# Loading the first x tile ahead of the weights, with the first products dealt out anew, in a fused convolution and two-matmul kernel

## The chip, the cores and the metric

The kernel runs on one core of one Trainium2 chip. The metric is device time in microseconds (us). A core has five engines that matter here: TensorE (PE in the profile, PEld for its weight loads), VectorE (DVE), ScalarE (ACT), GpSimd (POOL) and SyncE (SP), which issues most of the transfers. Times within a trace are microseconds from the start of the profiled execution, whose span is 1.7 to 2.1 us shorter than the time on the device in the runs here.

Before the change the median of three runs was 821.86 us (821.55 to 822.88).

## The reference, cut to what matters

```python
w = softmax(weight_gen, axis=-1)             # [8, 4096, 8 heads, 7 taps]
x_pad = pad x with 6 rows of zeros in front  # [8, 4096, 192] -> causal
conv[b, s, h] = sum over k of w[b, s, h, k] * x_pad[b, s + k, h]   # 24 channels per head
h = conv.reshape(32768, 192) @ w_in          # 192 -> 2048
out = (h - tanh(h)) @ w_out                  # 2048 -> 192
```

## The kernel before

The 32,768 tokens are cut into 32 superblocks of 1,024 tokens. For each superblock:

- a softmax of the tap weights (an exponential on ScalarE, sum and reciprocal on VectorE, a normalising product `wsm` on GpSimd);
- seven products of x with one tap each (`prod`, L146);
- transposes of these products on TensorE, which also add the seven taps up in PSUM (`pc`), and a copy to `convT` on ScalarE;
- 16 rounds, coded as 8 pairs, of a first matmul (`ph`, L192), a tanh on ScalarE and a subtraction on VectorE (`gt`, L203);
- the second matmul (`po`, L223), which runs one superblock behind.

"Body n" is below the loop's pass in which the first matmul of superblock n runs. The products of superblock n + 2 are made during body n. The parts that the change touches:

```python
    def products(n, on_vector=()):
        ...                                  # wsm on GpSimd
        for k in range(K):
            prod = ppool.tile([P, NC, J, H, GC], BF16, name=f"prod{k}", tag=f"prod{k}")
            eng = nc.vector if k in on_vector else nc.gpsimd
            eng.tensor_mul(prod..., x_t[:, k : k + J, :]..., wsm[:, :, :, k : k + 1]...)
    ...
    load(0)                                  # tap weights, then x, on SyncE's queue
    for h in range(H):                       # casts fp32 -> bf16, triggered by GpSimd
        nc.gpsimd.dma_start(out=w_in[h * GC : (h + 1) * GC], in_=moe_w_in...)
    softmax_exp(0)
    softmax_norm(0)
    products(0, on_vector=(1, 3, 5, 6))
    nc.sync.dma_start(out=w_in[R:P], in_=w_in[0:R])      # second copy, for the other half of the rows
    load(1)
    nc.gpsimd.dma_start(out=w_out[:], in_=moe_w_out...)
    softmax_exp(1)
    softmax_norm(1)
    conv(0, (0, 1))                          # transposes of superblock 0
    conv(0, (2,))
    products(1, on_vector=(2, 5))
    load(2)
    softmax_exp(2)
    softmax_norm(2)
    for n in range(NTOT):
        ...                                  # load(n + 3), products(n + 2)
        for p in range(J):
            gemm1(n, 2 * p)
            gemm1(n, 2 * p + 1)
            ...
            if n >= 1:
                gemm2((n - 1) * J + p)
            if n + 1 < NTOT:
                if p == (2 if n else 5):
                    conv(n + 1, (0, 1))
                if p == (5 if n else 6):
                    conv(n + 1, (2,))
            ...
```

x and the prods have two buffers each. Three PSUM buffers are shared by `ph` and `pc`.

The softmax here doesn't subtract the row's maximum and nothing guards it: scores larger than these inputs give would overflow.

## Time and profile before

| | before |
|---|---|
| time, median | 821.86 us |
| TensorE busy | 769.5 us, 94% of the span |
| GpSimd / VectorE / ScalarE busy | 82% / 81% / 78% |
| first x tile landed | 14.54 us |
| last product of superblock 0 | 29.55 us |
| first subtraction on VectorE | 38.98 us |
| GpSimd's last product of superblock 1 / of superblock 2 | 49.29 / 70.36 us |
| transposes of superblock 2 done | 70.95 us |

How to read it: an average over the whole span says "TensorE, 94%". That is true of bodies 2 to 31. It says nothing on the first 70 us, where TensorE waits for data. A change at the start can only move the point from which TensorE is full, and for this the question is what comes last there. "The transposes of superblock 2" means here and below the first of their two calls, `conv(2, (0, 1))`, which takes two thirds of the channels; the last third follows about 8 us later. The lines themselves are in the prediction below.

### The profile page before, as it was taken

The page shows a single profiled execution, that of the slowest core. Times are in us where ns is not written, and L with a number is a line of the kernel's source. Part 1 is how long each engine was busy: PE and PEld are TensorE (multiplying, and loading weights), DVE is VectorE, ACT ScalarE, POOL GpSimd, SP SyncE. Part 2 cuts the span into 40 slices and gives each one's busy share as a digit, 9 for nine tenths or more (in the row PEclk, how much of TensorE's full clock was granted, in tenths as well). Part 3 has the DMA queues.
Part 4 walks back from the last instruction along what each step waited for, and adds up shares of the span by engine and source line. Part 5 has one row for each costly group of instructions (what it writes and reads, how often), then busy time and mean ns, then how long its engine had stood idle before and what let it go on. Part 6 is the DMA issues. An engine that isn't in the chain of part 4 may idle for free.

```text
span 820.7 us, 35994 instructions
## 1 busy us (share of the span) xinstructions
PE 769.5 (94%) x16640; PEld 602.6 (73%) x16640; DVE 661.0 (81%) x591; ACT 640.1 (78%) x865; POOL 669.0 (82%) x265
## 2 busy tenths in 40 slices
PE   0379999999999999999999999999999999999997
PEld 0247777777778777777777777777777878777777
DVE  3987878888888887887888888888888888787783
ACT  0277778888888878888888888888888888888883
POOL 5999999998898888899888889988888898885000
PEclk9989999999999999999999999999999999999999
DMA  8823333233224323332333332233233223301112
GB/s 145 216 80 81 119 120 119 71 119 120 96 77 119 120 70 120 102 94 95 119 102 87 120 120 73 99 119 114 76 120 110 95 87 120 108 3 42 41 41 79
DMA packets 17286, 81.21 MB, mean 99 GB/s; under 512 B 4160, under 2 KB 8816, under 8 KB 12984
## 3 DMA queue, kind: packets, MB, share of 16 engines
q1 hardware_dynamic: 14560, 77.34, 28.2%
q0 software_dynamic: 2576, 1.57, 1.7%
q8 instruction: 130, 2.13, 1.1%
q14 instruction: 20, 0.16, 0.1%
HBM read 54.49 MB, written 25.17 MB: 97 GB/s over the span
## 4 chain that ended last, share of the span: by engine, by line
PE 79%; DVE 13%; ACT 4%; issue 2%; DMA 1%; SPq 0%; POOL 0%; ACTq 0%; DVEq 0%; POOLq 0%
PE ph L192 36%; PE po L223 35%; DVE gt L203 10%; PE pc L169 6%; ACT th L201 4%; DVE prod L146 3%; DMA x_t<-in_x_dram 1%; PE po L264 1%; DVE zr L129 0%; DVE zsum L125 0%; POOL wsm L136 0%; SPq L96 0%; ACT e_t L115 0%; SPq L100 0%; SPq L77 0%
## 5 line engine op out<-in xcount | busy, mean ns | idle before, releaser
L203 DVE TENSOR_TENSOR gt<-ph,th 128x1024 bf16<-128x1024 f32 x512 | 602.5, 1219 | 130.0 <-ACT th L201 130.0
L146 POOL TENSOR_TENSOR prod<-x_t,wsm 128x1536 bf16<-128x1536 f32 x218 | 632.6, 2939 | 78.0 <-issue 70.3
L201 ACT ACTIVATE th<-ph 128x1024 f32<-128x1024 f32 x512 | 496.9, 1022 | 58.3 <-PE ph L192 56.3
L192 PE MATMUL ph<-convT,w_in 64*128 64x512 bf16 x3072 | 393.1, 378 | 13.8 <-DVE gt L203 10.5
L223 PEld LDWEIGHTS <-gt 64*128 64x128 bf16 x7936 | 346.1, 94 | 54.4 <-issue 3.4
L223 PE MATMUL po<-w_out,gt 64*128 64x192 bf16 x7936 | 375.8, 243 | 4.2 <-issue 2.4
L192 PEld LDWEIGHTS <-w_in 64*128 64x128 bf16 x3072 | 171.3, 94 | 128.5 <-issue 38.1
L169 PE MATMUL pc<-ident,prod 64*128 64x64 bf16 x5376 | 93.7, 192 | 29.4 <-POOL prod L146 25.9
L169 PEld LDWEIGHTS <-prod 64*128 64x128 bf16 x5376 | 89.8, 96 | 31.2 <-POOL prod L146 26.2
L179 ACT ACTIVATE convT<-pc 128x1024 bf16<-128x1024 f32 x64 | 51.9, 810 | 65.0 <-PE pc L169 65.0
L248 ACT ACTIVATE out_sb<-po 128x192 f32<-128x192 f32 x248 | 82.5, 333 | 24.3 <-PE po L223 20.7
L115 ACT ACTIVATE e_t<-wg_t 128x448 f32<-128x448 f32 x32 | 18.5, 577 | 20.9 <-DMA wg_t<-in_weight_gen_dram 20.9
L136 POOL TENSOR_TENSOR wsm<-e_t,zr 128x448 f32<-128x448 f32 x32 | 31.1, 972 | 1.7 <-DVE zr L129 1.7
L146 DVE TENSOR_TENSOR prod<-x_t,wsm 128x1536 bf16<-128x1536 f32 x6 | 21.0, 3556 | 10.8 <-DMA x_t<-in_x_dram 9.6
L125 DVE TENSOR_REDUCE zsum<-e_t 128x64 f32<-128x448 f32 x32 | 19.5, 609 | 2.8 <-ACT e_t L115 2.8
L129 DVE RECIPROCAL zr<-zsum 128x64 f32<-128x64 f32 x32 | 17.7, 553 | 3.4 <-DVE zsum L125 0.5
L264 PE MATMUL po<-w_out,gt 64*128 64x192 bf16 x256 | 11.0, 243 | 0.0
L264 PEld LDWEIGHTS <-gt 64*128 64x128 bf16 x256 | 10.8, 93 | 0.0
L276 DVE TENSOR_TENSOR out_sb<-po,ot 128x192 f32<-128x192 f32 x8 | 2.9, 357 | 8.9 <-ACT ot L275 8.9
L275 ACT ACTIVATE ot<-po 128x192 f32<-128x192 f32 x8 | 2.6, 330 | 7.9 <-PE po L264 7.9
L292 POOL DMA_DIRECT2D w_in<-in_moe_w_in_dram x8 | 4.8, 604 | 0.4 <-issue 0.4
L115 ACT ACT_TABLE_LOAD x1 | 1.3, 1283 | 0.7 <-PEq L346 0.7
(8 smaller groups left out, 2.4 us busy)
## 6 DMA issues: line engine op xcount, KB each, us to landing
x_t<-in_x_dram SPq DMA_DIRECT2D x24, 1344.0 KB
out_dram<-out_sb SPq DMA_DIRECT2D x31, 768.0 KB
x_t<-in_x_dram SPq DMA_DIRECT2D x8, 1176.0 KB
wg_t<-in_weight_gen_dram SPq DMA_DIRECT2D x32, 224.0 KB
x_t<-in_x_dram SPq DMA_DIRECT2D x8, 157.5 KB
w_in<-in_moe_w_in_dram POOLq DMA_DIRECT2D x8, 96.0 KB, 11.2
w_in<-w_in SPq DMA_DIRECT2D x1, 768.0 KB
w_out<-in_moe_w_out_dram POOLq DMA_DIRECT2D x1, 768.0 KB, 13.0
```

The source lines that it names most:

```text
L115: nc.scalar.activation(out=e_t[:].rearrange("p j h k -> p (j h k)"), in_=wg_t[:].rearrange("p j h k -> p (j h k)"), func=ACT.Exp,)
L125: nc.vector.reduce_sum(out=zsum[:], in_=e_t[:].rearrange("p j h k -> p (j h) k"), axis=AX.X)
L136: nc.gpsimd.tensor_mul(wsm[:].rearrange("p j h k -> p (j h) k"), e_t[:].rearrange("p j h k -> p (j h) k"), zr[:].rearrange("p (n o) -> p n ...
L146: eng.tensor_mul(prod[:].rearrange("p c j h g -> p j h c g"), x_t[:, k : k + J, :].rearrange("p j (h c g) -> p j h c g", h=H, c=NC), wsm[: ...
L169: nc.tensor.matmul(pc[:, r, col : col + R], lhsT=prods[k][r * R : (r + 1) * R, c, 2 * j : 2 * j + 2].rearrange("p j h g -> p (j h g)"), rh ...
L179: nc.scalar.activation(out=convT[:, c0 : c0 + nch, :].rearrange("p c (j r t) -> p r (c j) t", r=2, t=R), in_=pc[:, :, 0 : nch * JH * R].re ...
L192: nc.tensor.matmul(ph[:, r, :], lhsT=w_in[r * R : (r + 1) * R, c, f * P : (f + 1) * P], rhs=convT[r * R : (r + 1) * R, c, :], start=(c == ...
L201: last_act[0] = nc.scalar.activation(out=th[:], in_=ph_f, func=ACT.Tanh)
L203: nc.vector.tensor_sub(gt[:], ph_f, th[:])
L223: mm = nc.tensor.matmul(po[:, 0:D], lhsT=g_of[n][f][r * R : (r + 1) * R, col : col + P], rhs=w_out[r * R : (r + 1) * R, f, :], start=(r == ...
L248: last_act[0] = nc.scalar.activation(out=out_sb[:, j, :], in_=po[:, 0:D], func=ACT.Copy)
L264: nc.tensor.matmul(po[:, r, 0:D], lhsT=g_of[n][f][r * R : (r + 1) * R, col : col + P], rhs=w_out[r * R : (r + 1) * R, f, :], start=(f == 0 ...
```

## The change

The intent is a shorter start. x of superblock 0 no longer moves beside w_in; GpSimd triggers w_in after its first product; the loads of superblock 1 go ahead of the copy of w_in to the other half of the rows; VectorE takes five instead of four of the first seven taps; to let VectorE start its subtractions sooner, all taps of superblock 1 go to GpSimd, and as they come later, the transposes of superblock 1 move behind the last pair of body 0. That copy of w_in is cut in two, so that its first half can start when half of w_in is there.

```diff
--- before.py
+++ after.py
@@ -129,7 +129,7 @@
         nc.vector.reciprocal(zr[:], zsum[:])
         zr_of[n] = (e_t, zr)
 
-    def products(n, on_vector=()):
+    def products(n, on_vector=(), between=None):
         x_t = x_of.pop(n)
         e_t, zr = zr_of.pop(n)
         wsm = wgpool.tile([P, J, H, K], FP32, name="wsm")
@@ -151,6 +151,8 @@
                 .to_broadcast([P, J, H, NC, GC]),
             )
             prods.append(prod)
+            if between is not None and k == 0:
+                between()
         prods_of[n] = prods
 
     def conv(n, chunks):
@@ -287,23 +289,29 @@
 
     ctx.enter_context(tc.manual_schedule())
 
+    def load_w_in():
+        for h in range(H):
+            nc.gpsimd.dma_start(
+                out=w_in[h * GC : (h + 1) * GC],
+                in_=moe_w_in[h * G : (h + 1) * G].rearrange("(c g) f -> g c f", c=NC),
+            )
+
     load(0)
-    for h in range(H):
-        nc.gpsimd.dma_start(
-            out=w_in[h * GC : (h + 1) * GC],
-            in_=moe_w_in[h * G : (h + 1) * G].rearrange("(c g) f -> g c f", c=NC),
-        )
     softmax_exp(0)
     softmax_norm(0)
-    products(0, on_vector=(1, 3, 5, 6))
-    nc.sync.dma_start(out=w_in[R:P], in_=w_in[0:R])
     load(1)
+    products(0, on_vector=(1, 3, 4, 5, 6), between=load_w_in)
+    for q in range(2):
+        nc.sync.dma_start(
+            out=w_in[R + q * R // 2 : R + (q + 1) * R // 2],
+            in_=w_in[q * R // 2 : (q + 1) * R // 2],
+        )
     nc.gpsimd.dma_start(out=w_out[:], in_=moe_w_out.rearrange("(c p) e -> p c e", c=NFT))
     softmax_exp(1)
     softmax_norm(1)
     conv(0, (0, 1))
     conv(0, (2,))
-    products(1, on_vector=(2, 5))
+    products(1)
     load(2)
     softmax_exp(2)
     softmax_norm(2)
@@ -320,9 +328,9 @@
             if n >= 1:
                 gemm2((n - 1) * J + p)
             if n + 1 < NTOT:
-                if p == (2 if n else 5):
+                if p == (2 if n else 7):
                     conv(n + 1, (0, 1))
-                if p == (5 if n else 6):
+                if p == (5 if n else 7):
                     conv(n + 1, (2,))
             if p == 2 and n + 3 < NTOT:
                 softmax_norm(n + 3)
```

## The prediction

> **What bounds the kernel now.** I read the page first, for what bounds the long middle; then the chain of waits, for where the start is lost; then GpSimd's timeline, because the change moves work to it; then stretches of the first 80 us with the granted clock.
>
> ```profile
> PE 769.5 (94%) x16640; PEld 602.6 (73%) x16640; DVE 661.0 (81%) x591; ACT 640.1 (78%) x865; POOL 669.0 (82%) x265
> PE   0379999999999999999999999999999999999997
> ```
>
> TensorE is above 90% busy from the fourth of 40 slices (20.5 us each) to the last but one. The change touches nothing after body 1 (the loop's pass for superblock 1), so it can only shift the point at which that full stretch begins. Only the first 60 to 70 us are at stake.
>
> ```profile
> 2.87 11.67 DMA x_t<-in_x_dram
> 14.67 14.88 DVE prod L146 x4
> 31.82 6.13 DVE prod L146 x2
> ```
>
> These are three pieces of the chain that ended last (start, length, what): the first x tile lands at 14.54, VectorE's four products of superblock 0 run until 29.55, and its two of superblock 1 until 37.95. The first subtraction on VectorE (gt) starts at 38.98. This is the stretch that the change attacks. But GpSimd runs beside it:
>
> ```profile
> 2.48 4.05 POOL L292 DMA_DIRECT2D w_in<-in_moe_w_in_dram  x7
> 14.70 13.24 POOL L146 TENSOR_TENSOR prod<-x_t,wsm 128x1536 bf16<-128x1536 f32 x3 [7.16 <-DMA x_t<-in_x_dram]
> 27.88 1.23 POOL L301 DMA_DIRECT2D w_out<-in_moe_w_out_dram  x1
> 30.82 0.96 POOL L136 TENSOR_TENSOR wsm<-e_t,zr 128x448 f32<-128x448 f32 x1 [1.72 <-DVE zr L129]
> 31.86 17.43 POOL L146 TENSOR_TENSOR prod<-x_t,wsm 128x1536 bf16<-128x1536 f32 x5
> 49.26 0.96 POOL L136 TENSOR_TENSOR wsm<-e_t,zr 128x448 f32<-128x448 f32 x1
> 50.30 20.06 POOL L146 TENSOR_TENSOR prod<-x_t,wsm 128x1536 bf16<-128x1536 f32 x7
> ```
>
> From 30.82 on GpSimd has no pause: products of superblock 1 end at 49.29, those of superblock 2 at 70.36. Who needs them is in TensorE's timeline:
>
> ```profile
> 69.14 1.81 PE L169 MATMUL pc<-ident,prod 64*128 64x64 bf16 x110
> 70.78 0.38 PE L192 MATMUL ph<-convT,w_in 64*128 64x512 bf16 x1
> ```
>
> The transposes of superblock 2 begin at 69.14 and end at about 70.95, and the seventh product came at 70.36. So today the GpSimd chain arrives just in time: it is missing from the chain of waits, but has no slack. From there on TensorE is full (8.57 busy of the next 8.60 us). My reading of the time: the end is fixed by when the transposes of superblock 2 are done.
>
> [...] a VectorE product took 1.757 us where it came first and 4.45 beside GpSimd; GpSimd's took 2.895 alone and 4.41 to 4.48 beside VectorE. Products on both engines simply take turns[...]. [...] TensorE was idle from 34.1 to 40.2, and
>
> ```profile
> 31.70:38.50 6.80, 2.17 (x20) 0.87 (x15) 6.66 (x3) 3.92 (x5) 6.72 (x3) 1.00 1.25 312
> 38.50:45.30 6.80, 5.10 (x24) 2.10 (x24) 6.28 (x6) 3.43 (x4) 6.80 (x3) 0.50 0.13 17
> ```
>
> (stretch, length, busy time of TensorE, its weight loads, VectorE, ScalarE, GpSimd, then granted clock, DMA share, GB/s): a whole 6.8 us at 0.50 followed. It cost little there because VectorE was the bound.
>
> **The change part by part.**
>
> *x ahead of w_in.* The same kind of x load (a first superblock of a batch, in three pieces) runs without w_in beside it at 71.62: the trace has its last landing at 79.34, 7.7 us later; the next such load is 155.88 to 163.63. The first one is issued at 2.50, so I expect it at about 9.8 to 10.1 and products from 9.95, against 14.67: 4.7 us earlier. Its packets took about 0.63 us each even without w_in, against 0.41 for the later 128-partition loads, so I don't use the faster rate.
>
> *Five products on VectorE, two on GpSimd, triggers between.* VectorE's first 9.95 to 11.7; GpSimd's first, blocked by it, to 14.46 (4.48 long). Then eight triggers of 0.58: 4.64, to about 19.15. VectorE meanwhile does its second (blocked, to 16.1) and two alone (to 19.4). [...] VectorE's fifth ends at 23.8. [...] End of superblock 0's products: 23.8 against 29.55, 5.75 us earlier.
>
> *GpSimd's chain.* The w_out trigger ends near 23.4; the normaliser of superblock 1 is ready at 23.8 + 1.2 = 25.0; wsm to 26.05; seven products all on GpSimd, 20.06 us (the row at 50.30), to 46.2. That is 20.06 instead of 17.43, 2.6 us longer than with VectorE's two. Then wsm and seven more: 67.25, against 70.36. Gain of this chain: 5.75 - 2.63 = 3.1 us.
>
> *TensorE and VectorE.* VectorE no longer has products of superblock 1 (6.13 us). w_in lands after the triggers, I estimate at 22.5 to 27 (its last six pieces needed from 9.2 to 16.8 in today's trace), and its copy to the other partition half 3.6 us after that, so the first matmuls with w_in start at 26.5 to 30 and the first gt near 30.5 to 33, 6 to 8.5 us earlier than 38.98. Putting the transposes of superblock 1 behind body 0 costs about what it costs now (pauses of 1.6 and 0.8 us in VectorE's timeline today, one of 2.5 us then), and is needed because products arrive only at 46.2. Body 1's first gt comes at about 30.5 + 22 = 52.5 instead of 61.5. Seven and a half microseconds later TensorE asks for superblock 2's products, at about 60, and they are complete only at 67.25.
>
> So of the 6 to 8.5 us won at the front, TensorE gives most back waiting in body 1 for GpSimd. Transposes of superblock 2 end at 67.5 instead of 70.95: 3.4 us earlier. That is the sum before the clock.
>
> *The clock.* TensorE would stand nearly idle for 3 to 7 us around 61 to 67, with some 0.2 us of transposes per product. A stop of 6 us today lost the full clock for 6.8 us. Here the recovery falls into the stretch where TensorE is the bound: 3.4 to 6.8 us at half clock lose 1.7 to 3.4. I give it 70 to 75%, so an expected loss of about 1.8. Net: 821.9 - 3.4 + 1.8 = about 820.2; I take 820.0.
>
> **The rivals.**
> 1. *The front gain survives whole* (6 to 8 us, 814 to 816). For it: the chain of waits names only x, VectorE's products and gt. Against it: GpSimd's 42 us for superblocks 1 and 2 have no slack. It needs products of superblock 2 by 61 to 63, and nothing in the change makes GpSimd that much faster.
> 2. *The wait costs the clock in full* (821 to 823, no gain). For it: the 0.50 stretch above. Against: [...] a late w_in shortens the pause.
> 3. *w_in becomes the bound.* Its triggers end 12.6 us later than now. Today pieces three to eight started moving 6 us after their triggers, for a reason that I can't read. Landing at 27 is still free, since body 0 may slip by up to 7 us before superblock 2's products wait for it; only past 30 would it cost.
> 4. *Triggers are slowed by VectorE's products.* [...] GpSimd's chain slips by up to 3 us and the gain is gone (822 to 824). [...] 15%.
> 5. *x lands at 8.5 to 9*, at the faster packet rate: 1 us better.
>
> **Range and chances.** Terms: -3.4 from the GpSimd chain (within 1 for the landing of x), +0 to +3.4 for the clock, tails for 3 and 4. 8 in 10: 816.5 to 823.0. A 2% change is 16.4 us, more than twice the whole front gain, so within 2% is almost sure.
>
> **What would show it.** Step by step in the profile after: products begin near 10; VectorE's fifth ends near 24; GpSimd's products of superblock 1 end near 46 and of superblock 2 near 67; VectorE's first gt near 31; a new wait of TensorE's transposes on GpSimd's products in body 1, of 3 to 7 us; a granted clock of 0.50 starting in or just after it. I am wrong if that wait is missing (then GpSimd was faster or TensorE slower than worked out), if the clock stays full (nearer 818), or if the chain of waits shows w_in or its copy ahead of the first gt with body 1 later than 60.

## The result, and the profile after

The changed kernel took 821.12 us (median of 4 runs, 819.33 to 822.39), against 822.37 for the kernel before in the same rounds (821.55 to 823.40). Ratios here are the mean time of one kernel's fast runs over that of the other's of the same rounds, so not quite the ratio of the medians quoted: 0.9983, with a 95% interval of 0.996 to 1.0006. So the change is worth about 1.4 us if anything. The predicted 820.0 us and its range (816.5 to 823.0) held; the prediction's gain of 1.9 us was near, but not for all of its reasons.

The page after: the first line is busy time by engine, the second TensorE's busy share by slice.

```profile
PE 772.2 (94%) x16640; PEld 605.3 (74%) x16640; DVE 655.8 (80%) x590; ACT 640.7 (78%) x865; POOL 665.8 (81%) x266
PE   0578899999999999999999999999999999999997
```

The second slice has 5 instead of 3 and the third 7 as before, but the fourth and fifth have 8 and 8 where before there was a 9. The start is earlier and then thinner: a first sign of a gain that is given back. The chain of waits after, with start, length and what was waited for (its longest pieces of the start):

```profile
2.86 6.82 DMA x_t<-in_x_dram
9.84 4.48 POOL prod L146
14.32 4.17 POOL w_in L294 x7
18.49 5.95 DMA w_in<-in_moe_w_in_dram
24.57 9.32 DMA w_in<-w_in
...
55.94 12.82 POOL prod L146 x5
```

Two things are new. The front of the chain now runs through w_in and its copy, until 33.9, and no longer through VectorE's products. And GpSimd's products, which were missing from the chain before, are in it from 55.94 to 68.76. GpSimd's own timeline after:

```profile
14.27 4.80 POOL L294 DMA_DIRECT2D w_in<-in_moe_w_in_dram  x8
19.09 2.92 POOL L146 TENSOR_TENSOR prod<-x_t,wsm 128x1536 bf16<-128x1536 f32 x1
21.94 1.23 POOL L309 DMA_DIRECT2D w_out<-in_moe_w_out_dram  x1
26.58 0.96 POOL L136 TENSOR_TENSOR wsm<-e_t,zr 128x448 f32<-128x448 f32 x1 [3.40 <-DVE zr L129]
27.61 20.06 POOL L146 TENSOR_TENSOR prod<-x_t,wsm 128x1536 bf16<-128x1536 f32 x7
47.63 0.97 POOL L136 TENSOR_TENSOR wsm<-e_t,zr 128x448 f32<-128x448 f32 x1
48.68 20.07 POOL L146 TENSOR_TENSOR prod<-x_t,wsm 128x1536 bf16<-128x1536 f32 x7
```

The products of superblock 2 end at 68.75 instead of 70.36. TensorE's timeline after, around the transposes of superblock 2 and at 100 us:

```profile
66.27 1.64 PE L171 MATMUL pc<-ident,prod 64*128 64x64 bf16 x96
68.81 0.41 PE L171 MATMUL pc<-ident,prod 64*128 64x64 bf16 x16 [0.90 <-POOL prod L146]
...
100.08 2.10 PE L225 MATMUL po<-w_out,gt 64*128 64x192 bf16 x23 [2.16 <-issue]
```

TensorE asks for superblock 2 at 66.27 (before: 69.14), waits 0.90 us for GpSimd's last product, and is done with the transposes at 69.2 instead of 70.95: 1.7 us won. At 97.9 it stops again for 2.16 us, with "issue" as the cause, which means that the profile shows no engine or transfer that it waited for. The stretches around this stop (length, busy time of TensorE, its weight loads, VectorE, ScalarE, GpSimd, granted clock, DMA share, GB/s):

```profile
97.90:99.90 2.00, 0.02 (x1) 0.00 (x0) 2.00 (x2) 0.75 (x1) 2.00 (x2) 1.00 0.36 134
99.90:103.30 3.40, 3.22 (x31) 2.68 (x33) 0.23 (x1) 0.33 (x1) 3.40 (x2) 0.50 0.03 9
```

After the stop came 3.4 us at half clock. The kernel before had such a stop too, until 101.53, without the half clock; in its chain of waits it is this piece:

```profile
99.61 1.92 issue
```

VectorE's seventh subtraction of body 2 started at 97.12 before and 95.42 after, 1.7 us earlier; its first of body 3 at 113.33 and 113.44. So in these two executions the whole gain was lost between 95 and 113 us. The spans still differ by 1.0 us (820.7 and 819.7), since pauses and body lengths of later bodies also vary by some tenths from one execution to the next. The record has the mean granted clock of every execution. For the four of the changed kernel it is 0.998 (the profiled one, 821.43 us), 1.000 (820.82), 0.997 (822.39) and 1.000 (819.33), so two of the four had some half clock and two had none. (An estimate from the span of 819.7 us: a mean that rounds to 1.000 leaves room for at most 0.8 us of half clock.)

### The profile page after: what moved, and what is told of

Read it like the earlier page. It is cut to its first block, busy times and chain, and to the rows that moved or that the text cites. A ratio compares the mean times of both kernels' runs of the same rounds, so it can differ in the third digit from the quotient of the medians.

```text
span 819.7 us, 35995 instructions
## 1 busy us (share of the span) xinstructions
PE 772.2 (94%) x16640; PEld 605.3 (74%) x16640; DVE 655.8 (80%) x590; ACT 640.7 (78%) x865; POOL 665.8 (81%) x266
## 4 chain that ended last, share of the span: by engine, by line
PE 78%; DVE 11%; ACT 4%; DMA 3%; POOL 3%; issue 1%; SPq 0%; POOLq 0%; DVEq 0%
PE ph L194 36%; PE po L225 35%; DVE gt L205 10%; PE pc L171 6%; ACT th L203 4%; POOL prod L146 2%; PE po L266 1%; DMA w_in<-w_in 1%; DMA x_t<-in_x_dram 1%; DMA w_in<-in_moe_w_in_dram 1%; POOL w_in L294 1%; SPq L96 0%; DVE zr L129 0%; DVE zsum L125 0%; SPq L77 0%
## 5 line engine op out<-in xcount | busy, mean ns | idle before, releaser
L194 PEld LDWEIGHTS <-w_in 64*128 64x128 bf16 x3072 | 173.1, 94 | 129.4 <-issue 33.7
L250 ACT ACTIVATE out_sb<-po 128x192 f32<-128x192 f32 x248 | 82.7, 333 | 25.9 <-PE po L225 22.4
L146 DVE TENSOR_TENSOR prod<-x_t,wsm 128x1536 bf16<-128x1536 f32 x5 | 15.5, 3162 | 4.7 <-DMA x_t<-in_x_dram 4.7
```

Source lines behind the costliest of these rows:

```text
L146: eng.tensor_mul(prod[:].rearrange("p c j h g -> p j h c g"), x_t[:, k : k + J, :].rearrange("p j (h c g) -> p j h c g", h=H, c=NC), wsm[: ...
L194: nc.tensor.matmul(ph[:, r, :], lhsT=w_in[r * R : (r + 1) * R, c, f * P : (f + 1) * P], rhs=convT[r * R : (r + 1) * R, c, :], start=(c == ...
L250: last_act[0] = nc.scalar.activation(out=out_sb[:, j, :], in_=po[:, 0:D], func=ACT.Copy)
```

## The experiments

Eleven kernels ran. Theory A is the prediction's, put more sharply after the trace was read: the time is set by when TensorE has the transposes of superblock 2 behind it, and that is the later of two chains, GpSimd's products and the front (w_in, its copy, VectorE's subtractions of body 0). The rivals: the front alone sets it, as the chains of waits suggest in both kernels (B); or something else holds body 1 (C). The runs fell on three chips, on which the kernel before had medians of 821.31 (e1 to e4), 822.23 (b1, b2, e5, e6) and 820.40 us (e7 to e9). So times of different groups are compared by their ratios to the kernel before. All results were correct.

### b1: the kernel before, with products of superblock 1 all on GpSimd

```diff
-    products(1, on_vector=(2, 5))
+    products(1)
-                if p == (2 if n else 5):
+                if p == (2 if n else 7):
-                if p == (5 if n else 6):
+                if p == (5 if n else 7):
```

> The kernel before, with only two parts of the change: all seven products of superblock 1 on GpSimd, and the transposes of superblock 1 last in body 0. Theory A (the end is set by the later of GpSimd's chain and the front): VectorE's first subtraction comes near 34 instead of 39, but GpSimd's products of superblock 2 end near 73.0 instead of 70.36, so TensorE waits some 8 us for them in body 1, and the time is 2.5 us longer, and 2 to 3.4 us more where the pause costs the full clock: 824 to 827. Rival B (the chain of waits of the kernel before names VectorE's two products and the first subtraction): about 5 us shorter, 816 to 817.

Measured: 824.89 us (4 runs, 824.65 to 825.91), ratio 1.0035 (1.0022 to 1.0048). VectorE's first subtraction moved from 38.98 to 33.80, 5.2 us earlier, and the kernel became 2.9 us slower. GpSimd's products of superblock 2 ended at 72.70. TensorE's timeline in this run:

```profile
65.98 1.46 PE L169 MATMUL pc<-ident,prod 64*128 64x64 bf16 x80
69.89 0.41 PE L169 MATMUL pc<-ident,prod 64*128 64x64 bf16 x16 [2.45 <-POOL prod L146]
72.75 0.61 PE L169 MATMUL pc<-ident,prod 64*128 64x64 bf16 x16 [2.45 <-POOL prod L146]
```

TensorE asks at 65.98 and takes the last two taps as GpSimd delivers them, 2.9 us apart, idle for 4.9 us in all (some 8 were expected). The granted clock was then 0.50 from 70.3 to 77.1. This run decides against B: it took away exactly what the chain of waits of the kernel before names (VectorE's two products, 6.13 us), and lost time, because GpSimd's chain had no slack. It also shows that this part of the change by itself costs time.

### b2: the kernel before, with only the order of the loads changed

```diff
     load(0)
-    for h in range(H): ...                      # w_in triggers
     softmax_exp(0)
     softmax_norm(0)
-    products(0, on_vector=(1, 3, 5, 6))
-    nc.sync.dma_start(out=w_in[R:P], in_=w_in[0:R])
     load(1)
+    products(0, on_vector=(1, 3, 5, 6), between=load_w_in)   # after tap 0
+    nc.sync.dma_start(out=w_in[R:P], in_=w_in[0:R])
```

> The kernel before, with only the order of the loads changed: x of superblock 0 (and of superblock 1) ahead of w_in, whose triggers follow one GpSimd product; taps and transposes where they were before. Theory A: products of superblock 0 end near 24, GpSimd's products of superblock 2 near 67, first subtraction near 36, transposes of superblock 2 done near 68 instead of 70.95: about 3 us shorter than before (818.5), so most of what the whole change could give. Rival B (the parts need each other): no better than the changed kernel, 821.

Measured: 818.83 us (5 runs, 818.12 to 819.98), ratio 0.9961 (0.9949 to 0.9973). The interval excludes 1: this one part is worth about 3.2 us (822.1 x 0.0039). By the point values that is more than twice the whole change, but the interval overlaps the changed kernel's (0.996 to 1.0006). GpSimd's products of superblock 2 ended at 67.32, the first subtraction started at 35.94, and the transposes of superblock 2 were done at 68.75. Products of superblock 0 ended at 26.5, not near 24: VectorE's fourth took 8.96 us, from 17.55 to 26.51, and both GpSimd products that stood behind the triggers ran first, from 19.11 to 24.88 (see e7).

### e3: the changed kernel, with taps 2 and 5 of superblock 1 back on VectorE

```diff
-    products(1)
+    products(1, on_vector=(2, 5))
```

> The changed kernel, with taps 2 and 5 of superblock 1 back on VectorE, as before the change. Theory A: VectorE does them while it would wait for w_in's copy (from about 27.6 to 33.8), so its first subtraction stays near 36.5; GpSimd's products of superblock 2 end 2.6 us earlier, near 66.1, and the time is about 1.2 us shorter (820). Rival B (VectorE is the bound of the start, as the chain of waits of the kernel before says): 3 to 6 us longer.

Measured: 817.83 us (5 runs, 817.32 to 818.77), ratio 0.9959 (0.9943 to 0.9976). VectorE made the two products from 27.57 to 33.71, while it would have waited anyway; its first subtraction started at 35.84 instead of 36.50. GpSimd's products of superblock 2 ended at 66.12, and the transposes were done at 67.7 without a wait:

```profile
65.85 1.81 PE L171 MATMUL pc<-ident,prod 64*128 64x64 bf16 x110
```

By the point values the gain over the changed kernel (0.9983) is larger than the 1.2 us expected, though the intervals overlap: the trace has 1.5 us at the transposes, and no half clock from 38 us on. The rival, which expected 3 to 6 us more, falls.

### e2: the changed kernel, with six first taps on VectorE

```diff
-    products(0, on_vector=(1, 3, 4, 5, 6), between=load_w_in)
+    products(0, on_vector=(1, 2, 3, 4, 5, 6), between=load_w_in)
```

> The changed kernel, with six of the seven first taps on VectorE, so that no GpSimd product stands behind the w_in triggers. Theory A: products of superblock 0 end at about 22.7 instead of 25.3, GpSimd's products of superblock 2 at about 66.1 instead of 68.75, the copy of w_in still lands near 34 and the first subtraction still starts near 36.5; TensorE no longer waits for superblock 2, and the time is about 1.2 us shorter (820). Rival B (w_in and its copy set the end): no change.

Measured: 817.69 us (5 runs, 817.26 to 818.78), ratio 0.9958 (0.994 to 0.9977). Products of superblock 0 ended at 22.70, GpSimd's of superblock 2 at 66.14, both as expected; transposes were done at 67.0 without a wait. Again the gain is above the expected 1.2 us, because the copy of w_in came 1.4 us earlier too (w_out's transfer began and ended earlier), and its trace has no half clock from 38 us on. Two different edits that each shorten GpSimd's chain by 2.6 us give the same time, and in both traces TensorE's wait is gone: it was GpSimd's chain that came last in the changed kernel. How much of the time that explains is less sure, since the intervals of e2 and e3 overlap the changed kernel's and the front came earlier in both, too (1.4 and 0.7 us at the first subtraction).

### e1: the changed kernel, with the w_out trigger later

```diff
-    nc.gpsimd.dma_start(out=w_out[:], in_=moe_w_out...)
...
-    products(1)
+    products(1, between=load_w_out, at=2)       # after GpSimd's third product
```

> The changed kernel, with the w_out trigger moved behind the third GpSimd product of superblock 1. Theory A (the end is set by when the transposes of superblock 2 are done, and that by the later of two chains: GpSimd's products, and the front chain of w_in, its copy and VectorE's subtractions): the second half of the w_in copy no longer starts 4 us late behind w_out's small descriptors, lands near 29 instead of 33.9, and the first subtraction starts near 32 instead of 36.5; TensorE asks for superblock 2 near 62 instead of 66.3 but GpSimd's products, with the trigger now in their way, end near 70 instead of 68.75. Time about 1 us longer than the changed kernel (822), or 2 to 4 us longer if the longer wait costs TensorE its full clock. Rival B (the chain of waits is right that w_in and its copy set the end): 4 to 5 us shorter, about 816.

Measured: 821.98 us (5 runs, 820.76 to 822.79), ratio 1.0007 (0.999 to 1.0024). Waits in the first 37 us of the changed kernel and then of this run (engine, what it waited for, total us, times, longest):

```profile
PE ph L194 <- DMA w_in<-w_in: 6.1, 1, 6.1
```

```profile
PE ph L194 <- DMA w_in<-w_in: 0.8, 1, 0.8
```

The copy of w_in landed 5.2 us earlier and the first subtraction started at 31.26 instead of 36.50. The packet records say why: the second half of the copy was issued at 24.57 in the changed kernel, and its first packet moved at 29.16, while w_out's 2,048 descriptors (the pieces into which a transfer is cut, each one record of 384 bytes in the trace) ran from 24.59 on, 1,241 of them by 29.16; without w_out beside it that half was issued at 24.02 and moved from 25.20 on. So the delay from issue to first packet was 4.6 us with w_out beside it and 1.2 us without. That w_out caused the delay is shown; how the two transfers took turns is not.

And the 5 us were worth nothing, while GpSimd's chain, with the trigger in it, ended 1.3 us later. The waits and one stretch around the transposes of superblock 2 in this run:

```profile
PE pc L171 <- POOL prod L146: 6.9, 3, 2.5
```

```profile
67.50:74.30 6.80, 4.36 (x56) 2.54 (x50) 1.20 (x1) 3.03 (x3) 6.72 (x4) 0.50 0.31 76
```

TensorE asked at 61.22, waited 6.9 us in three pieces for GpSimd, whose last product came at 70.06, and then ran at half clock until 74.3. B, which expected 816, falls here a second time. The half clock after a long trickle of transposes, which the prediction feared for the change itself, did come once the pause was as long as it had assumed. The record has clocks of 0.993 to 0.996 for all five executions, so none of them escaped it.

### e4: the three edits together

The edits of e1 (trigger behind tap 4), e2 and e3.

> The three edits together: w_out trigger late (behind tap 4 of superblock 1), six first taps on VectorE, taps 2 and 5 of superblock 1 on VectorE. Theory A: GpSimd's products of superblock 2 end near 64.5 to 65, first subtraction near 32, TensorE asks for superblock 2 near 62, its transposes done near 65: about 4 us shorter than the changed kernel (817), up to 3 us less of a gain if the pause costs the full clock. Rival B (front alone): about 5 us shorter.

Measured: 817.27 us (6 runs, 815.04 to 817.57), ratio 0.9947 (0.9931 to 0.9964). Its trace: first subtraction 32.02, TensorE asks at 61.35, waits 1.73 us, transposes done at 65.1, no half clock from 32 us on, span 813.1. The profiled execution is the fastest (815.04); the five others took 817.0 to 817.6. A half clock doesn't explain these 2 us: two of the five (817.55 and 817.03) have a recorded clock of 1.000 as well. They left no trace, so the cause stays open.

### e5: the changed kernel, with later transposes in bodies 1 and 2

```diff
-                if p == (2 if n else 7):
+                if p == (7, 4, 4)[n] if n < 3 else p == 2:
-                if p == (5 if n else 7):
+                if p == (7, 6, 6)[n] if n < 3 else p == 5:
```

> The changed kernel, with the transposes of superblock 2 (and 3) after the fifth and seventh pair of body 1 (and 2) instead of the third and sixth: no work is added or taken from an engine. Theory A: TensorE's pause on GpSimd's products in body 1 disappears, the stretch from there on is as before: 1 to 2 us shorter than the changed kernel (819 to 820), and with no half clock in the first 110 us. Rival C (the pause is harmless, something else holds body 1): no change.

Measured: 820.16 us (6 runs, 818.60 to 822.58), ratio 0.9984 (0.997 to 0.9999): no better than the changed kernel's 0.9983. In its trace the wait for GpSimd in body 1 is gone, and body 3 begins at 111.15 instead of 113.44. But that is the fastest of its six executions (818.60), and the others spread over 3 us. A miss in the time, and the time is what rival C expected: the pause of 0.90 us is too small to be found among what varies between executions. It is not the half clock that varies: all six executions have a recorded clock of 1.000. What does is left open.

### e6: the three edits and the later transposes

> The three edits of the earlier run with all three (late w_out trigger, six first taps on VectorE, taps 2 and 5 of superblock 1 on VectorE) plus the later transposes of superblocks 2 and 3. Theory A: the front's whole gain survives; no pause of TensorE in body 1 and no half clock: about 3.5 us shorter than with the three alone in its undisturbed run, so 812 to 814. Rival C: no better than 817.

Measured: 816.43 us (5 runs, 815.15 to 817.86), ratio 0.9931 (0.9919 to 0.9944). By the point values better than e4 (0.9947), with overlapping intervals, and short of the 812 to 814 expected. The trace shows body 1 without a wait for GpSimd, and then, at 94.1, a stop of 1.91 us with "issue" as its cause, and half clock from 96.8 to 100.3:

```profile
92.66 1.47 PE L171 MATMUL pc<-ident,prod 64*128 64x64 bf16 x89
96.04 0.52 PE L171 MATMUL pc<-ident,prod 64*128 64x64 bf16 x23 [1.91 <-issue]
```

It is the same stop as at 97.9 in the changed kernel and at 99.6 in the kernel before. All traces but those of e8 and e9 have one between 93 and 104 us, of 0.64 to 2.16 us. Half clock stood behind some of them only: behind 2.16 us in the changed kernel (0.50 from 99.9 to 103.3) and 1.91 us in e6, but not behind 1.92 us in the kernel before. In e1 it came behind 6.3 us (61.2 to 67.5) in which TensorE was busy for 1.85 us, and lasted 6.8 us. What decides is not settled here.

The packet records show one thing at that point in the traces of these three. An instruction fetch (the queue that the page calls "instruction", one packet of 16,384 bytes) ends 1.2 to 1.5 us before TensorE goes on: at 100.08 in the kernel before (TensorE at 101.53), 98.62 in the changed kernel (100.08), 94.85 in e6 (96.04). In these traces the fetch began only when the x load of superblock 5 was through and part of superblock 0's output store, issued right behind it, had been moved (x packets from 92.44 to 98.28 in the kernel before and from 90.85 to 96.73 in the changed kernel, the store's first at 97.44 and 96.05, the fetch at 99.11 and 97.66). The page of the profile counts 130 such packets, and TensorE ran twice 16,640 instructions, 256 for each packet; that nearly all of these fetches are TensorE's is an estimate from these counts.

### e8 and e9: the output store of superblock 0 held back

e8 is e6 and e9 the changed kernel, each with this edit:

```diff
-    opool = ctx.enter_context(tc.tile_pool(name="opool", bufs=2))
+    opool = ctx.enter_context(tc.tile_pool(name="opool", bufs=3))
...                                              # in the loop, after load(n + 3)
+        if n == 3:
+            store(0, held.pop())                # was issued in body 2, behind the x load
```

> The run with all three edits and later transposes, with the output store of superblock 0 held back until the x load of superblock 6 has been issued (and a third output buffer for it). It asks about TensorE's pause of 1.9 us near 94. Theory F (TensorE there waits for its own instructions[...]): the pause falls under 0.7 us, no half clock near 97, time 813 to 815 instead of 816.4. Rival (the pause comes with the place in the program, whatever the transfers): unchanged, 816.4.

> The changed kernel with only that store held back. Theory F: the pause of 2.2 us near 98 and the half clock behind it go, and the 1.7 us that body 1 had won over the kernel before survive: 818 to 819.5. Rival: unchanged, 821.

Measured: e8 814.58 us (5 runs, 814.52 to 815.47), ratio 0.9928 (0.9915 to 0.994); e9 818.64 us (5 runs, 817.73 to 819.40), ratio 0.9975 (0.9962 to 0.9988). TensorE's timeline of e8, where e6 had stopped for 1.91 us and then had half clock:

```profile
91.33 1.50 PE L233 MATMUL po<-w_out,gt 64*128 64x192 bf16 x32
92.65 1.81 PE L171 MATMUL pc<-ident,prod 64*128 64x64 bf16 x112
94.28 1.48 PE L194 MATMUL ph<-convT,w_in 64*128 64x512 bf16 x12
```

No wait stands behind any of them, and the fetch began at 91.62 instead of 93.84 (in e9 at 95.83 instead of 97.66 in the changed kernel). The seventh subtraction of body 2 started at 89.47 in e8 and at 89.48 in e6; the first of body 3 at 105.12 and 108.88, so 3.8 us were saved in between. In e9 the stop and the half clock are gone as well: the same two points are 95.67 and 109.93, against 95.42 and 113.44 in the changed kernel. So what makes the stop is shown for these traces: with this transfer of 768 KB moved away the fetch comes earlier (2.2 us in e8, 1.8 in e9) and the stop is gone. What the fetch waits for in the DMA engines is in no record. How much of it the median keeps is not. The medians lie in the expected ranges, but on a chip on which the kernel before was faster, too (820.40). By the ratios e8 (0.9928) and e6 (0.9931) do not differ, nor do e9 (0.9975) and the changed kernel (0.9983) beyond their intervals. In e8's trace another stop with "issue" as its cause, 1.54 us, stands at 342 us, and body 3, with one of 0.74 us at 117, is 1.0 us longer than in e6. Which executions have how many of these stops stays open.

### e7: the w_in triggers behind GpSimd's second product

```diff
-    products(0, on_vector=(1, 3, 4, 5, 6), between=load_w_in)
+    products(0, on_vector=(1, 3, 4, 5, 6), between=load_w_in, at=2)
```

> The changed kernel, with the w_in triggers behind GpSimd's second product instead of its first. It asks why VectorE's fourth product took 6.10 us in the changed kernel. Theory L [...]: with no GpSimd product behind the triggers no VectorE product takes over 4.5 us, and the fifth ends near 23.7 instead of 25.3. Rival T (the triggers themselves hold VectorE up): a VectorE product beside the triggers again takes longer than its 1.75 us alone. In both w_in lands 4 us later, near 29, first subtraction near 40, and the time is 1 to 3 us longer than the changed kernel (822 to 824).

Measured: 822.04 us (4 runs, 820.98 to 822.60), ratio 1.0012 (0.9996 to 1.0027), as both theories expected: by the ratios 2.4 us longer than the changed kernel, though the intervals overlap. VectorE's products of superblock 0, first in the changed kernel and then in this run:

```profile
9.80 15.50 DVE L146 TENSOR_TENSOR prod<-x_t,wsm 128x1536 bf16<-128x1536 f32 x5 [4.72 <-DMA x_t<-in_x_dram]
```

```profile
9.78 13.85 DVE L146 TENSOR_TENSOR prod<-x_t,wsm 128x1536 bf16<-128x1536 f32 x5 [4.52 <-DMA x_t<-in_x_dram]
```

13.85 us is what turns without a gap would give. In the trace before, four VectorE and three GpSimd products by turns took 14.88 us, and one of each 4.4; from these a turn of VectorE's is about 1.68 us and one of GpSimd's 2.72 (estimates), and five and two of them make 13.84. In the changed kernel one VectorE product took 6.10 us, from 17.53 to 23.63, although GpSimd's second product is shown only from 19.09 to 22.01, 1.56 us later, and triggers ran before it. Theory L says that this GpSimd product, standing behind the triggers, held VectorE up before its own record begins. In e7 the products beside the triggers took 1.75 us, and the triggers 0.58 us each, as they did without a product beside them, so triggers do not hold VectorE up here (rival T falls). With no GpSimd product queued behind the triggers nothing was lost (theory L stands), nor in e2, where the VectorE products that began beside the triggers took 1.75 us. With two queued, in b2, VectorE lost its turn twice, 8.96 us in all: there the engines did not simply take turns, as the prediction has it. That the queued product is what holds VectorE up is the reading that fits; by what means is in no record.

## Why the prediction was right or wrong

**x ahead of w_in: right.** Expected at 9.8 to 10.1, landed at 9.68. The estimate came from a later load of the same kind.

**Five products on VectorE, two on GpSimd: right in kind, 1.5 us too short.** That the products of the two engines take turns without a gap failed: VectorE's fourth ran from 17.53 to 23.63, although GpSimd's second began only at 19.09, and the fifth product ended at 25.30 instead of 23.8. e7 removed the loss.

**GpSimd's chain: right, with that 1.5 us carried through.** Superblock 1 at 47.68 instead of 46.2, superblock 2 at 68.75 instead of 67.25. The 20.06 us for seven products was exact. So the chain gained 1.6 us and not 3.1.

**The front: wrong in size.** "The first gt near 30.5 to 33" was 36.50, because the copy of w_in took until 33.9. The step that failed is "its copy to the other partition half 3.6 us after that": the second half took 9.3 us, held up by w_out's small descriptors. e1 removed this, and the first subtraction came at 31.26, inside the range. Rival 3, w_in as a bound, was thus closer than I had it. w_in itself landed at 24.44, inside the expected 22.5 to 27.

**TensorE gives most back waiting for GpSimd: the mechanism was right, the size was not.** The wait was 0.90 us and not 3 to 7, since TensorE asked at 66.27 and not near 60. That is the copy of w_in again: the first subtraction was 6.0 us later than the 30.5 of the sum, body 0 took 22.4 us (22 expected), and 7.4 us later (7.5 expected) TensorE asked. GpSimd was only 1.5 us later than expected, so both chains, not one, ended near 68 us. b1 and e1, which have the early front, show waits of 4.9 and 6.9 us and no gain.

**The clock: wrong in place.** The expected loss of 1.8 us "around 61 to 67" did not occur; the clock stayed full there. Of the 3.4 to 6.8 us at half clock that the prediction reckons with, the trace before shows the upper figure (38.5 to 45.3), and the lower came in the changed kernel (99.9 to 103.3); its 70 to 75% was the author's estimate. In the profiled execution 1.8 us more than in the kernel before were lost near 98 to 103, for a reason that the prediction did not have: a stop of 2.16 us for an instruction fetch (gone in e9, where the fetch began 1.8 us earlier), and a half clock of 3.4 us behind it. So the size of the sum came out near the truth partly by chance: 1.7 us won at the transposes instead of 3.4, and a loss of the assumed size from another cause. Two of the four executions have a recorded clock of 1.000 and did not have that half clock (820.82 and 819.33 us). Of the three signs of being wrong that the prediction names, two came: the clock stayed full at body 1, and the copy of w_in stands in the chain ahead of the first gt, though body 1 began at 58.86 and not after 60.

**The chance of within 2%: right,** as the front gain is a fraction of 16 us.

What the change was worth by its parts: the order of the loads alone, about 3 us (b2, 0.9961); all products of superblock 1 on GpSimd, a loss (b1, 1.0035; undone in e3, 0.9959). b2, with four first taps on VectorE and the copy in one piece, and e3, with five and the copy in two, are equal within their intervals. By these point values the change bought about 3 us with its first part and gave about half of it back with its last one, which was there to free VectorE, at a time when VectorE had become free anyway. How much it gave back is not settled by the times, as the interval of the whole change overlaps those of b2 and e3; in the traces e3 is 1.5 us earlier than the changed kernel at the transposes of superblock 2, b2 0.5 us.

The best version run is e8, 0.9928 of the time before, about 5.9 us; its interval (0.9915 to 0.994) lies below the changed kernel's. It can't be told from e6 (0.9931).

## What to carry to other kernels

A chain of waits names what came last, not what comes second; before work is moved off the named engine, look for the chain that ends just before it, because that one becomes the bound (b1: the front 5.2 us earlier, the kernel 2.9 us slower). When a start is shortened, move work to whichever engine will be waiting in the new order, and keep transfers of many small pieces out of the way of the one that is waited for (e1: the copy of w_in landed 5.2 us earlier without w_out's 2,048 pieces of 384 bytes beside it). With differences of 1 to 2 us, look in the trace at fixed points of the program, since the medians also contain stops that come and go.
